# One output tile's wo product, taken in two banks at different times, and x's tiles loaded last

## The chip, the core and the metric

The kernel runs on 1 core of a Trainium2 chip. A core has TensorE (PE, matmuls; PEld are its weight loads), VectorE (DVE), ScalarE (ACT), GpSimd (POOL) and SyncE (SP), which here only issues DMAs. Matmul results go to PSUM, which has eight banks of 512 f32 columns; all else is in SBUF. The metric is the device time of one execution in microseconds (us), the median over runs; lower is better.

## The reference

A transformer block with adaptive layer norm. D = 640, 2048 rows, 32 heads of 128, a key/value cache of 2048 rows, all bf16:

```python
mod = (_silu(c) @ w_mod).reshape(c.shape[0], 6, 1, -1)      # sa, ca, ga, sb, cb, gb
h = _layernorm(x) * (1 + ca) + sa
x = x + ga * _A_ref(h, k_cache, v_cache, wq, wo)    # softmax attention, 32 heads, then @ wo
h = _layernorm(x) * (1 + cb) + sb
x = x + gb * _B_ref(h, w1, w2, w3, w4)              # x1 = x + shift4(gelu(LN(x) @ w1)) @ w2
                                                    # x1 + gelu(LN(x1) @ w3) @ w4
```

`_A_ref` projects queries with `wq`, takes softmax(q k^T / sqrt(128)) v for each head, and multiplies the 4096 concatenated values of a row by `wo` (4096 x 640). That last product, for the first rows, is what the change is about.

## The kernel before

**Planner.** Every operation is recorded by `Prog` with the tiles it reads and writes; it works out the semaphore waits. The order on each engine and on each DMA queue is the order in which the operations are recorded. A DMA that waits holds up all that stands behind it on its queue (nearly all are on SP's).

**The attention loop.** `NG` = 512 units: unit s is head s // 16, query tile s % 16 (128 rows). The loop's step s has two halves (1024 keys each). In step s, PE makes the scores of unit s (`qk`, L357 and L15: two 512-column matmuls a half, into half of `Sps`), and the product with V of unit s - 10 (`pv`, L371: eight matmuls a half). DVE copies the scores with a running minimum (L703), POOL joins the two minima (L708), ACT takes the exponential into a slot of `ring` (L711). The scores must be transposed before `pv`. Most units go three at a time (a trio) through one DMA transpose on SP (`transpose`, L286); the last trios are 491-493, 494-496, 498-500, 501-503, 504-506 and 507-509, sent at steps 493, 496, 500, 503, 506 and 510. Some units, among them 490, 497, 510 and 511, are transposed on PE instead (`t_piece`, L324: two 128x128 f32 transposes a half step, into one of the banks `JB[0]` = `Oaug` and `JB[1]` = `QPp`, or into `Sps` for 510 and 511), and ACT copies each 512-column half of the unit back to the ring (`t_evac`, L331). `PE_AT` gives the step where this starts: 501 for unit 497, and its two halves (r = 0, 1) take steps 501 and 502. The same two banks serve the query projection of the next head (`q_piece`, L301), whose last piece is in step 493.

**Values out and back.** Two units' PV results are copied by ACT (L688), normalized by POOL (L548, L555) and stored for four units at once to `o_scratch` in HBM by POOL's queue (L562). For the output product they are read back transposed: `load_ot` (L604) on SP brings a pair of query tiles, heads h0 to h1, into `OTj[pair % 2]`. Pair 0 (tiles 0 and 1) comes in four parts (`ot0(i)`, heads `OTC[i]` to `OTC[i + 1]`); parts 0, 1 and 2 are issued at the steps `OTS`, part 3 (the last head) at step 513. In step 493 and others, `ot0` of the first entry stands ahead of that step's trio on SP, the later entries behind it. `OTj[0]` lies on `hTx`, which holds the projection's input until step 493; `OTj[1]` lies on `negS`, DVE's score buffer, so pair 1 comes after the loop's last exponential.

**Output product.** Tile j's row block is `sum over heads of O_h @ wo_h`: 32 matmuls of 512 columns and 32 of 128 (`NC2`). `y0(h0, h1)` (L647) does a range of heads of tile 0 in the banks `Oaug` (512 columns) and `QPp` (128); `y1` does tile 1 in the first half of `Sps` (`a_pe`, L636). `TAIL` puts them into the loop: before, heads 0 to 15 of tile 0 go one per half step from step 504 to 511, both column parts; heads 16 to 30, and heads 0 to 30 of tile 1, follow in one block in step 513. After step 525 PE does head 31 of both tiles, then tile 2 (`a_two`, first heads 0 to 15 of pair 1, then the rest), tile 3 and so on. DVE takes each tile out of its bank (`a_s1`: L762 the product with ga, L764 the sum with x, then statistics L754, L756) and goes on with `a_s2` (L770, L773). Even tiles use the second half of `Sps`, odd ones the first.

**Loads of x.** x's 16 tiles are read again into `xt` (`load_xt`, L615): four tiles (640 KB) in step 513, between the two halves of pair 1; twelve (1920 KB) in step 522.

Of the kernel before, what the change touches and what calls it, by code (L numbers as in the profile page):

```python
# [123 lines left out]
def bass_adaLN_cond__mha_block_cached__mixer_s_mlp__prompt_kernel(  # L124
# [3 lines left out]
    _, H, SK, DH = A_k_cache.shape  # L128
# [11 lines left out]
    NG = H * NQT  # L140
# [3 lines left out]
    NC2 = [(0, 512), (512, D - 512)]  # L144

    with ExitStack() as es:
# [9 lines left out]
        if True:  # L156
            with ExitStack() as es1:
# [4 lines left out]
                PE_AT = {32 * i + t: 32 * i + a for i in range(NG // 32) for t, a in PE_T.items()}  # L162
# [97 lines left out]
                for s in range(NG):  # L260
                    end = s >= NG - 10
                    g = s - PVD
# [6 lines left out]
                    if s in first_of:  # L269
                        m = first_of[s]  # L270
                        a = take([13] if m is trios[-1] else WIN[0:3] if end else WIN)
                        for i, g in enumerate(m):
                            PSL[g] = a + i
                    if s in last_of:
                        m = last_of[s]
                        a = take([7] if m is trios[-1] else WIN[3:6] if end else WIN)
# [15 lines left out]
                def bank(key):  # L292
                    if key not in bank_of:
                        bank_of[key] = jbank[0] % 2
                        jbank[0] += 1
                    return bank_of[key]
# [14 lines left out]
                def t_bank(g, r):  # L311
                    if g >= NG - 2:
                        return Sps[:, (2 + r) * 512:(3 + r) * 512], [("S", 1), ("Sb", 2 + r)]
                    jb = bank(("t", g, r))
                    return JB[jb], [("J", jb)]

                def t_piece(g, r, q):
# [17 lines left out]
                for h in range(H):  # L335
                    pieces = {}
                    u = 2 * NQT * h
# [7 lines left out]
                    PIECES.append(pieces)  # L345

                def t_of(s):
                    return [(g, s - a) for g, a in PE_AT.items() if a <= s < a + 2]

                def qk(s, half):  # L350
                    h, j = divmod(s, NQT)
# [48 lines left out]
                for i, (n0, n1) in enumerate(MROW):  # L400
# [8 lines left out]
                     r=["id0"] + WOR, w=["ident"])  # L409
# [4 lines left out]
                     r=["c", "ident"] + WOR, w=[("J", 0)])  # L414
# [188 lines left out]
                def load_ot(pr, h0=0, h1=H, part=0):  # L603
                    G.dma("sync", lambda e: e.dma_start_transpose(  # L604
                        OTj[pr % 2][:, 2 * h0:2 * h1, :], o_scr[pr, :, h0:h1].rearrange("q h z d -> q (h z d)")),
                          ("ot", pr % 2, part), r=[("osd", pr // 2, hh) for hh in range(h0, h1)],
                          w=[("OT", pr % 2, i) for i in ([part] if pr == 0 else (part, 2)[:part + 1] if h1 - h0 < H else range(3))]
                          + ([("OTa", 0)] if pr == 2 and part == 0 else [])
                          + (HTK if pr == 0 and part == 3 else NEG if pr == 1 and part == 0 else []))

                def ot0(i):
                    load_ot(0, OTC[i], OTC[i + 1], OTP[i])

                def load_xt(c0, c1):
                    G.dma("sync", lambda e: e.dma_start(  # L615
                        xt[:, 4 * c0:4 * c1], x2d[c0 * 512:c1 * 512, :].rearrange("(t p) d -> p t d", p=128)),
                        ("xt", c0), w=[("x1", t) for t in range(4 * c0, 4 * c1)] + ringk(XT0 + 4 * c0 * D, XT0 + 4 * c1 * D))

                OTC = [0, H // 4, H // 2, H - 1, H]
                OTP = [3, 0, 1, 2]  # L620
                yn = [0]

# [17 lines left out]
                         w=[("S", b)] + ([("Sb", 2), ("Sb", 3)] if b == 1 else []))  # L640
                    return b

                def y0(h0, h1):
                    def f(t):
                        for jb, (c0, cw) in enumerate(NC2):
                            for hh in range(h0, h1):
                                ins = t.matmul(JB[jb][:, 0:cw], OTj[0][:, 2 * hh, :], wo[:, hh, c0:c0 + cw],  # L647
                                               start=(hh == 0), stop=(hh == H - 1))
                        return ins
                    G.op("tensor", f, r=[("OT", 0, OTP[i]) for i in range(4) if OTC[i] < h1 and h0 < OTC[i + 1]] + [("OTa", 0), "wo", "woz", "wo4"],  # L650
                         w=[("J", 0), ("J", 1)])

                def y1(h0, h1):
                    a_pe(1, 0, [OTP[i] for i in range(4) if OTC[i] < h1 and h0 < OTC[i + 1]], (h0, h1))
# [4 lines left out]

                YB = [Sps[:, 0:1024], Sps[:, 1024:2048]]  # L660
                LAG = 4
                Y0S = NG - 8
                OTS = [NG - 16, NG - 16, NG - 8]
                TAIL = {(s, z): [(y0, 2 * (s - Y0S) + z, 2 * (s - Y0S) + z + 1)] for s in range(Y0S, NG) for z in range(2)}
                TAIL[(NG + 1, 1)] = [(y0, OTC[2], OTC[3]), (y1, 0, OTC[3])]
                for s in range(NG + PVD + LAG):
                    h, j = divmod(s, NQT)
                    g_ = s - PVD
# [17 lines left out]
                    if 0 <= g_ < NG and g_ % 2 == 1:  # L686
# [3 lines left out]
                            r=[("O", p % 2)], w=[("Of", p % 4)])  # L690
# [4 lines left out]
                    for half in range(2):  # L695
                        if s < NG:
# [3 lines left out]
                            if is_pe(s):  # L700
# [5 lines left out]
                                r=[("S", half)], w=[("negS", s % 3), ("nmh", half, r8)])  # L706
                    if s < NG:
                        G.op("gpsimd", lambda g, r8=r8: g.tensor_scalar(  # L708
                            out=nm[:, r8:r8 + 1], in0=nm0[:, r8:r8 + 1], scalar1=nm1[:, r8:r8 + 1], scalar2=None, op0=ALU.min),
                            r=[("nmh", 0, r8), ("nmh", 1, r8)], w=[("nm", r8)])  # L710
                        G.op("scalar", lambda a, s=s, r8=r8: a.activation(  # L711
                            ring[:, PSL[s], :], negS[:, s % 3, :], ACT.Exp, bias=nm[:, r8:r8 + 1], scale=-1.0),
                            r=[("negS", s % 3), ("nm", r8)], w=slot(PSL[s]))
# [16 lines left out]
                    if 0 <= s - PVD - LAG:  # L730
                        gr, z = divmod(s - PVD - LAG, 4)
# [3 lines left out]
                    if s == NG + PVD - 9:  # L735
                        G.op("gpsimd", lambda g: g.memset(mhalf, -0.5), w=["mhalf"] + NEG)
                        ot0(3)
                        load_ot(1, 0, H // 2, 0)
                        load_xt(0, 1)
                        load_ot(1, H // 2, H, 1)  # L740
                    if s == NG + PVD:
                        load_xt(1, NQC)
                GELU = ACT.Gelu_apprx_tanh
# [273 lines left out]
```

## Time and profile before

| | us |
|---|---|
| median of 3 runs (1527.22 to 1528.97) | 1527.29 |
| the profiled execution | 1526.63 |
| its span on the core | 1524.8 |
| PE busy | 1489.2 (98%) |
| DVE busy | 1370.3 (90%) |
| ACT busy | 1256.8 (82%) |
| POOL busy | 625.9 (41%) |
| stretch 1190 to 1208: PE, DVE busy | 18.00, 18.00 |
| stretch 1208 to 1238: PE, DVE busy | 29.38, 6.40 |
| stretch 1238 to 1340: PE, DVE busy | 101.67, 69.99 |

Times within the execution count from the span's start. The granted TensorE clock was 1.00 throughout. In the timeline a row is start, length, engine, line, operation, what it writes and reads, and how many; a wait stands at its end in brackets. Lengths of PE rows overlap, since matmuls are pipelined: the price of one is the distance from start to start. Rows of SPq are the issuing of a DMA; when its data has landed is told apart (us from the issue). The chain of waits gives start, length, and what the time went to.

Step 504 begins on PE at 1189.92, step 501 at 1183.06. The last exponential begins at 1209.80, the block of heads 16 to 30 at 1211.00.

### The profile page before, as it was taken

Reading aid. Unit: us, or ns where it says so; the run is one execution under the profiler, and the core shown is the slowest. Engines: PE = TensorE matmul, PEld = TensorE weight load, DVE = VectorE, ACT = ScalarE, POOL = GpSimd, SP = SyncE. Lnnn points to the kernel's source line nnn. Section 1 sums busy time; section 2 is a strip of 40 time slices with the busy share of each in tenths; the row PEclk is TensorE's granted clock in tenths of the full one; section 3 lists DMA queues with packets and bytes.
Section 4 is the critical chain, followed back from the end, with each engine's and each line's share of the span. In section 5 each row is a group of like instructions: output and inputs, shape, how many; then the busy total and the mean of one; then the engine's idle time right before and its main releaser. Section 6 shows DMA issues by size and latency. Waiting matters only on the chain.

```text
span 1524.8 us, 32718 instructions
## 1 busy us (share of the span) xinstructions
PE 1489.2 (98%) x13702; PEld 917.9 (60%) x12678; DVE 1370.3 (90%) x2426; ACT 1256.8 (82%) x1182; POOL 625.9 (41%) x1402
## 2 busy tenths in 40 slices
PE   6899999999999999999999999999999999999999
PEld 3466666666666666666666666666666665554545
DVE  8999999999999999999999999999999756767425
ACT  6999999999999999999999999999999700034230
POOL 1244444444444444444444444444444433333000
PEclk9999999999999999999999999999999999999999
DMA  9999999999999999999999999999999998524101
GB/s 328 251 236 236 244 249 238 241 243 238 242 249 232 240 242 242 231 249 238 241 250 229 239 238 254 233 247 230 254 238 237 252 253 185 130 86 105 35 22 35
DMA packets 1155264, 330.29 MB, mean 217 GB/s; under 512 B 1133290, under 2 KB 1149738, under 8 KB 1155114
## 3 DMA queue, kind: packets, MB, share of 16 engines
q1 hardware_dynamic: 1146624, 307.09, 100.3%
q0 software_dynamic: 6144, 16.79, 3.4%
q10 hardware_dynamic: 2346, 4.34, 0.8%
q8 instruction: 103, 1.69, 0.5%
q14 instruction: 47, 0.39, 0.1%
HBM read 43.48 MB, written 19.40 MB: 41 GB/s over the span
## 4 chain that ended last, share of the span: by engine, by line
ACT 73%; PE 17%; DVE 5%; DMA 2%; issue 1%; SPq 1%; POOL 0%; DVEq 0%
ACT ring L711 60%; PE Sps L636 8%; ACT ring L331 5%; ACT Of L688 4%; ACT kv L308 4%; PE Sps L954 3%; DVE negS L703 3%; PE Oaug L905 2%; PE QPp L905 2%; PE Sps L890 1%; DMA negS<-o_scratch 1%; SPq L286 1%; DMA kv<-Of 1%; SPq L604 0%; ACT hTx L473 0%
## 5 line engine op out<-in xcount | busy, mean ns | idle before, releaser
L703 DVE TENSOR_SCALAR_CACHE_REDUCE negS<-Sps 128x1024 f32<-128x1024 f32 x1024 | 1173.9, 1223 | 8.2 <-PE Sps L15 7.3
L711 ACT ACTIVATE ring<-negS,small 128x2048 bf16<-128x2048 f32 x512 | 1116.7, 2372 | 2.1 <-POOL small L708 1.9
L371 PEld LDWEIGHTS PTp<-kv,ring 128*128 128x128 bf16 x8192 | 558.1, 98 | 295.0 <-issue 76.1
L371 PE MATMUL PTp<-kv,ring 128*128 128x129 bf16 x8192 | 645.0, 220 | 5.7 <-DMA ring<-ring 5.7
L357 PE MATMUL Sps<-kv 128*128 128x512 bf16 x1024 | 395.6, 386 | 9.0 <-DVE negS L703 4.6
L708 POOL TENSOR_SCALAR small<-small 128x1 f32<-128x1 f32 x512 | 146.1, 285 | 595.7 <-DVE negS L703 595.6
L15 PE MATMUL Sps<-kv 128*128 128x512 bf16 x1024 | 388.7, 380 | 0.0
L555 POOL TENSOR_SCALAR On<-Of,small 128x128 bf16<-128x128 f32 x512 | 190.1, 372 | 13.0
L688 ACT COPY Of<-PTp 128x259 f32<-128x259 f32 x256 | 186.3, 728 | 3.9 <-PE PTp L371 3.9
L357 PEld LDWEIGHTS Sps<-kv 128*128 128x128 bf16 x1024 | 98.3, 96 | 134.5 <-DVE negS L703 92.4
L548 POOL TENSOR_TENSOR small<-Of,small 128x4 f32<-128x4 f32 x128 | 133.1, 1040 | 13.7 <-ACT Of L688 13.5
L301 PE MATMUL Oaug<-hTx,kv 128*128 128x512 bf16 x315 | 119.0, 380 | 4.4 <-DMA kv<-in_A_wq_dram 2.6
L301 PE MATMUL QPp<-hTx,kv 128*128 128x512 bf16 x325 | 121.8, 381 | 0.9 <-ACT ring L331 0.8
L562 POOL DMA_DIRECT2D o_scratch<-On x128 | 103.8, 811 | 40.8 <-POOL On L555 37.2
L703 DVE DVE_READ_ACCUMULATOR negS<-Sps 128x1 f32 x1024 | 88.6, 87 | 0.0
L835 ACT ACT_TABLE_LOAD x1 | 1.3, 1283 | 105.9 <-POOL hTx L853 105.9
L331 ACT COPY ring<-QPp 128x512 f32<-128x512 f32 x78 | 74.9, 960 | 0.0
L331 ACT COPY ring<-Oaug 128x512 f32<-128x512 f32 x78 | 74.4, 954 | 0.0
L747 POOL TENSOR_SCALAR negS<-negS 128x1 f32<-128x1 f32 x48 | 24.3, 506 | 117.8 <-DVE negS L756 117.7
L636 PE MATMUL Sps<-wo,negS 128*128 128x128 bf16 (+1 forms) x512 | 71.5, 299 | 1.0 <-DMA negS<-o_scratch 1.0
L958 DVE TENSOR_TENSOR ring<-Sps,ring 128x640 f32<-128x640 f32 x15 | 12.4, 824 | 59.5 <-PE Sps L954 59.5
L308 ACT CAST kv<-QPp 128x512 bf16<-128x512 f32 x65 | 61.0, 938 | 1.4 <-PE QPp L301 1.4
(108 smaller groups left out, 1073.3 us busy)
## 6 DMA issues: line engine op xcount, KB each, us to landing
kv<-in_A_v_cache_dram SPq DMA_DIRECT2D x32, 512.0 KB, 5.2
o_scratch<-On POOLq DMA_DIRECT2D x128, 128.0 KB, 5.4
kv<-in_A_wq_dram SPq DMA_DIRECT2D x32, 160.0 KB, 3.5
wo<-in_A_wo_dram SPq DMA_DIRECT2D x1, 5120.0 KB, 21.5
ring<-in_A_x_dram SPq DMA_DIRECT2D x5, 640.0 KB, 5.1
ring<-in_w_mod_dram SPq DMA_DIRECT2D x5, 640.0 KB, 8.5
out_dram<-wo SPq DMA_DIRECT2D x15, 160.0 KB, 1.8
ring<-ring SPq DMA_TRANSPOSE x144, 9.6
```

The costliest lines, as they stand in the source:

```text
L15: return t.add_instruction(mybir.InstMatmult(name=t.bass.get_next_instruction_name(), ins=[t.lower_ap(rhs), t.lower_ap(lhsT)], outs=[t.low ...
L301: G.op("tensor", lambda t: t.matmul(JB[jb], wq[:, hb, q, :], hT[:, q, cc * 512:(cc + 1) * 512], start=(q == 0), stop=(q == KT - 1)), r=[(" ...
L331: G.op("scalar", lambda a: a.copy(dst, src), r=keys[-1:], w=[("PT", TSL[g], r)])
L357: ins = (t.matmul if c2 == 0 else partial(same_weights, t))(Sps[:, col:col + 512], QT[:, hb, j * 128:(j + 1) * 128], KTs[:, hb, col:col + ...
L371: ins = t.matmul(ob[:, 0:129], pt, Vaug[:, hb, kt, 0:129], start=(kt == 0), stop=(kt == NKT - 1))
L548: G.op("gpsimd", lambda g: g.tensor_tensor(out=rl[:, 4 * b:4 * b + 4], in0=Of[:].rearrange("p a z d -> p (a z) d")[:, 4 * b:4 * b + 4, 128 ...
L555: G.op("gpsimd", lambda g: g.tensor_scalar(out=On[:, b, z, :], in0=Of[:, 2 * b + z // 2, z % 2, 0:128], scalar1=rl[:, 4 * b + z:4 * b + z ...
L636: ins = t.matmul(YB[b][:, c0:c0 + cw], OTj[pr % 2][:, 2 * hh + z, :], wo[:, hh, c0:c0 + cw], start=(hh == 0), stop=(hh == H - 1))
L688: G.op("scalar", lambda a, p=p: a.copy(Of[:, p % 4].rearrange("p z d -> p (z d)")[:, 0:259], PO[:, (p % 2) * 512:(p % 2) * 512 + 259]), r= ...
L703: G.op("vector", lambda v, half=half, dst=dst, src=src, r8=r8: v.tensor_scalar(out=dst, in0=src, scalar1=-SCALE, scalar2=None, op0=ALU.mul ...
L708: G.op("gpsimd", lambda g, r8=r8: g.tensor_scalar(out=nm[:, r8:r8 + 1], in0=nm0[:, r8:r8 + 1], scalar1=nm1[:, r8:r8 + 1], scalar2=None, op ...
L711: G.op("scalar", lambda a, s=s, r8=r8: a.activation(ring[:, PSL[s], :], negS[:, s % 3, :], ACT.Exp, bias=nm[:, r8:r8 + 1], scale=-1.0), r= ...
```

## The change

- Tile 0's sums run at different times in the two banks. The 512-column part takes heads 0 to 23, one per half step, in steps 499 to 510; the 128-column part takes heads 0 to 13, one per half step, in steps 505 to 511. The block in step 513 then does heads 14 to 23 of the 128-column part, heads 24 to 30 of both, and heads 0 to 30 of tile 1.
- `OTC` cuts pair 0 into 16, 8, 7 and 1 heads (before: 8, 8, 15 and 1). Part 0 is issued at step 493 (before 496), part 1 at 496, part 2 at 504 as before.
- Since `Oaug` is taken from step 499 on, unit 497 uses `QPp` alone: its first half is transposed in step 501, the second in step 503 (before: 501 and 502, in two banks).
- On SP, pair 1's second half is issued before x's first four tiles.

```diff
                 def t_bank(g, r):
                     if g >= NG - 2:
                         return Sps[:, (2 + r) * 512:(3 + r) * 512], [("S", 1), ("Sb", 2 + r)]
-                    jb = bank(("t", g, r))
+                    jb = 1 if g == NG - 15 else bank(("t", g, r))
                     return JB[jb], [("J", jb)]
...
                 def t_of(s):
-                    return [(g, s - a) for g, a in PE_AT.items() if a <= s < a + 2]
+                    return [(g, (s - a) // (1 + (g == NG - 15))) for g, a in PE_AT.items()
+                            if s in ((a, a + 2) if g == NG - 15 else (a, a + 1))]
...
-                OTC = [0, H // 4, H // 2, H - 1, H]
+                OTC = [0, H // 2, 3 * H // 4, H - 1, H]
...
-                def y0(h0, h1):
+                def y0(h0, h1, jbs=(0, 1)):
                     def f(t):
-                        for jb, (c0, cw) in enumerate(NC2):
+                        for jb in jbs:
+                            c0, cw = NC2[jb]
                             for hh in range(h0, h1):
...
-                         w=[("J", 0), ("J", 1)])
+                         w=[("J", jb) for jb in jbs])
...
-                Y0S = NG - 8
-                OTS = [NG - 16, NG - 16, NG - 8]
-                TAIL = {(s, z): [(y0, 2 * (s - Y0S) + z, 2 * (s - Y0S) + z + 1)] for s in range(Y0S, NG) for z in range(2)}
-                TAIL[(NG + 1, 1)] = [(y0, OTC[2], OTC[3]), (y1, 0, OTC[3])]
+                OTS = [NG - 19, NG - 16, NG - 8]
+                YU = (2 * NG - 26, 2 * NG - 14)
+                TAIL = {divmod(u, 2): [(y0, u - YU[i], u - YU[i] + 1, (i,)) for i in range(2) if 0 <= u - YU[i] < OTC[2]]
+                        for u in range(YU[0], 2 * NG)}
+                TAIL[(NG + 1, 1)] = [(y0, 2 * NG - YU[1], OTC[2], (1,)), (y0, OTC[2], OTC[3]), (y1, 0, OTC[3])]
...
                         load_ot(1, 0, H // 2, 0)
+                        load_ot(1, H // 2, H, 1)
                         load_xt(0, 1)
-                        load_ot(1, H // 2, H, 1)
```

## The prediction

> **What bounds the kernel now.** The page first: ACT falls to 7 tenths in slice 32 of 40 and to 0 in 33 to 35, while PE stays at 9, so the attention loop ends near 1210 us and a PE-bound part follows. The edit lies around that seam, so I read the chain of waits there.
>
> ```profile
> 1203.51 2.32 DVE negS L703 x4
> ...
> 1213.95 6.50 SPq L286
> 1220.51 1.25 SPq L604
> 1221.81 5.70 SPq L604
> 1228.18 10.11 DMA negS<-o_scratch
> 1238.33 102.32 PE Sps L636 x752
> ```
>
> To be seen: DVE (the score copies) sets the loop's pace to its end; then SP's queue of DMA transposes carries the chain up to pair 1's second half, and at 1238.33 it hands over to PE, whose 752 matmuls follow without a hole. So time is won only if PE gets to that point sooner, which needs both PE and the transposes. Next the timeline of PE.
>
> ```profile
> 1183.97 0.39 PE L324 MATMUL Oaug<-identf,ring 128*128 128x128 f32 x2
> ...
> 1190.83 0.38 PE L647 MATMUL Oaug<-wo,hTx 128*128 128x512 bf16 x1
> 1191.05 0.22 PE L647 MATMUL QPp<-wo,hTx 128*128 128x128 bf16 x1
> ...
> 1211.00 3.40 PE L647 MATMUL Oaug<-wo,hTx 128*128 128x512 bf16 x15
> 1214.23 1.00 PE L647 MATMUL QPp<-wo,hTx 128*128 128x128 bf16 x15
> ...
> 1232.87 4.51 PE L636 MATMUL Sps<-wo,negS 128*128 128x512 bf16 x32
> 1238.33 7.97 PE L636 MATMUL Sps<-wo,negS 128*128 128x512 bf16 x48 [0.95 <-DMA negS<-o_scratch]
> ```
>
> To be seen: durations overlap, so prices are start-to-start. 15 matmuls of 512 columns take 3.23 us (1211.00 to 1214.23), 0.215 each; of 128 columns 0.84, 0.056 each. From 1189.92 to 1237.38 PE has no hole; then it waits 0.95 for pair 1. Last, SP's queue and two lines of DVE.
>
> ```profile
> 1168.45 0.58 SPq L231 DMA_DIRECT2D kv<-in_A_v_cache_dram  x1
> 1171.58 6.33 SPq L286 DMA_TRANSPOSE ring<-ring  x1
> 1177.95 2.59 SPq L604 DMA_TRANSPOSE hTx<-o_scratch  x1
> 1180.64 6.24 SPq L286 DMA_TRANSPOSE ring<-ring  x1
> 1186.92 2.47 SPq L604 DMA_TRANSPOSE hTx<-o_scratch  x1
> ...
> 1202.46 4.34 SPq L604 DMA_TRANSPOSE hTx<-o_scratch  x1
> ...
> 1227.55 0.58 SPq L615 DMA_DIRECT2D ring<-in_A_x_dram  x1
> 1228.18 6.07 SPq L604 DMA_TRANSPOSE negS<-o_scratch  x1
> ```
>
> ```profile
> 1233.72 0.83 DVE L764 TENSOR_TENSOR ring<-ring 128x640 bf16<-128x640 f32 x1
> 1243.48 0.89 DVE L773 SCALAR_TENSOR_TENSOR ring<-ring,negS,mod_bc 128x640 f32<-128x640 f32 x1 [4.31 <-DMA ring<-in_A_x_dram]
> ```
>
> To be seen: SP is free from 1169.03 to 1171.58 (it waits for step 493's exponential) and then issues back to back up to 1234.9. x's first transfer (L615) stands ahead of pair 1's second half.
>
> **Part 1, the sums in the loop.** A half step on PE is two score matmuls 0.44, eight PV 0.465, together 0.905. Two transposes of a PE tile add 0.23 (1183.97 to 1184.20), a 512-column sum 0.215, a 128-column one 0.05. DVE takes 1.145 for a half (2.29 a step). Before, steps 501 and 502 have transposes (1.135, under DVE), 503 nothing, 504 to 511 both sums (1.17: PE bound, 0.025 late each half; after 14 halves PE has used up its lead of 0.36 and DVE first starts 0.02 late, at 1206.97).
> After: 499 and 500 hold one 512 sum, 1.12 a half, still under 1.145, so DVE hides these four (0.86 us of PE work that leaves the full stretch). Steps 501 and 503 hold transposes and a sum, 1.35: 0.41 late each; 502 and 504 give back 0.05 each; 505 to 510 lose 0.025 twelve times. Sum 0.41-0.05+0.41-0.05+0.30 = 1.02, less the lead of 0.36: DVE ends the loop about 0.65 later. PE itself, which is then never idle from step 501 on, is the count that matters: from 1183.06 (score of 501) to 1237.38 it had 0.51 us of holes (6.86 us for steps 501 to 503, against 6.35 of work). These go, and the 0.86 goes: PE reaches pair 1's second half 1.37 sooner, at 1236.0. The bulk at 1211 loses eight 512 matmuls (1.72) and gains two of 128 (0.11).
>
> The 0.215 is this trace's row. The Trainium skill, TensorE: Matmul & The Clock Gate, section Back-to-back issue gap, gives about 131 ns for a matmul of 512 columns in a stream with weight loads; by it the four that leave would be worth 0.52, and the time 0.34 us more. Its isolated gap of 216 ns is the one that this trace shows.
>
> **Part 2, tile 497 in one bank.** Its second half is transposed at step 503 in place of 502, in the bank that its first half used. PE then waits for ACT's copy: that of the first half begins at 1186.72 and takes 0.6, PE comes at 1188.9: 1.6 of room. The second copy stands ahead of the exponential of 503 (1191.7), the first 128-column sum comes at 1193.9. ACT has these copies two steps apart, with work of 2.0 and 0.6 against two steps of 2.29. Tile 497 is read at step 507. ACT's slack hides it, cost 0; without that cover PE, which paces here, would pay each us in full.
>
> **Part 3, SP's queue.** Same number of transfers; 16, 8, 7 heads for 8, 8, 15. The first is issued at 493, ahead of the trio 491 to 493, as soon as PE's last projection (1166.80) is done: at 1169.1. No row has 16 heads there: 5.0 us by twice 2.5, 6.07 by the row of pair 1. I take 5.0, the same source and tile. The trio then starts at 1174.1, 2.5 late. That trio landed 7.9 us after its issue, others in this stretch 8.7 to 9.7; its transfer runs behind another, so I take 9.4: 1183.5. Tile 491's PV want it at 1183.50. Between the ends (1182.0, and 1184.9 with 6.07 and 9.7) the stall is 0 to 1.4, at the taken value 0. It would be paid in full, as PE is behind from there on. The next trio starts at 1180.5 as before (1180.64). From step 500 on SP is 0.3 early, after the 7 heads (2.1 for 4.34) 2.5 early. Nothing else gates it: exponential 509 ends at 1207.8 with the 0.65, SP comes at 1211.4. POOL's store of head 31 (issued 1211.10, landed 1216.16) moves with DVE to 1216.8, SP wants it at 1218.1.
> The sums' inputs: 16 heads land by 1169.1+5.0+2.8 = 1176.9 (8 heads landed 2.7 to 3.4 after the issue's end), the first sum is at 1179.4; the 8 by 1192.7 for 1198; the 7 by 1207 for 1211.7.
>
> **Part 4, x last.** Pair 1's second half goes 0.63 ahead of x: with the 2.5, issued at 1225.1 and landed 7.6 (first half) to 10.1 us (its own row) later: 1232.7 to 1235.2. Both are under PE's 1236.0, so the 0.95 wait goes too. x is issued at 1231.2 and lands 4.4 us later at the least (1235.6), at most 9.0 (the large x transfer): 1240.2. DVE's first add (L764, 1233.72 before) waits; behind it in DVE's order are tile 0's statistics and the product that frees tile 1's bank, 2.7 us in all (1233.72 to 1236.40), and PE's tile 3 waits for that bank, at 1238.33+4.4-2.3 = 1240.4. So x may land up to 1237.7 for nothing. Nearest row: x landed 2.5 after the transposes ahead of it (1231.96 after 1229.45), here 1235.2 to 1237.7. Cost 0; ends 0 and 2.5. The large x transfer follows at 1231.8, 2.5 sooner than 1234.35, so the 4.31 wait on DVE does not grow.
>
> **Sum.** PE passes 1238.33 at 1236.0: -2.3 us (1.37 + 0.95). Then the loop over tiles is PE's (DVE waits 32.2 us for PE in it), so it reaches the end. Profiled execution 1526.63 (span 1524.8) to 1524.3; the median shown, 1527.29, lies 0.66 above, so 1525.0.
>
> **Rivals.**
> - Trio late: the stall of part 3, up to 1.4. For it, no margin at the taken values; against, the one trio issued after a pause landed in 7.9. Time 1525.7 (1525.2 to 1526.4). Chance 0.14.
> - Transposes set the end: SP's gain is eaten by the transfers themselves (from 1174 to 1178 packets move at 290 GB/s without a gap, so the queue may be held by the engines), and pair 1 comes only 0.63 sooner. 1526.7. Chance 0.10.
> - The other side, x too late: mechanism of part 4. At 1240.0 all is given back, from 1243.1 it is slower by 0.2%. For it, 1920 KB follow 0.6 us behind on the same queue; against, the 4.4 row. At 9.0: 1527.5; if the two x transfers share the engines to the end (2560 KB in 13.4 us by 4.4 and 9.0), x lands at 1244.6 and the time is 1531.9. The Trainium skill, DMA: Bandwidth & Descriptors, section Queues, rings and completion order, says each DMA engine takes descriptors in ring order; by that rule x waits for pair 1 but not for the large transfer, and the landings 1229.45, 1231.96, 1238.29, 1243.36 in the order of issue agree. Chance 0.12, of which 0.07 beyond 0.2%.
> - More gain: PE's later holes (0.5 on a transposed tile and 0.2 on ACT, in the mixer) close as well: 1524.3 or less. For it, both hang on DVE's pace in the tiles; against, they lie 140 us on, behind work that PE paces. Chance 0.12.
> - The forecast, 1525.0 (1524.4 to 1525.7): 0.52.
>
> **Numbers.** 0.2% is 3.05 us, about what a measurement here can tell from none; so the forecast itself is "same". Faster needs 1524.24: 0.08 of the 0.12 for more gain, and 0.11 of the forecast by the spread of runs (1527.22 to 1528.97): 0.19. Slower: 0.07 from x, and 0.06 from the first two rivals should they meet and a run lie high: 0.13. Same 0.68. The range 1524.0 to 1527.6 leaves out about 0.06 below and 0.12 above.
>
> **What would show it.** Sums into Oaug from step 499 (about 1179), steps 501 and 503 longer by 0.4 on PE, DVE's last score copy near 1208.8; 16 heads in one L604 of about 5 us before the trio of 493; the bulk sums at 1211 with 7 and 17 matmuls; no wait on pair 1; L764 waiting for x instead of L773. Wrong, if PE shows a hole at tile 491 or 494, or before tile 3, or if the time after tile 2 changes.

## The result and the profile after

| | before | after |
|---|---|---|
| median of 20 runs each, on one chip (us) | 1527.73 | 1530.64 |
| ratio, 95% interval | | 1.0015 [1.0008, 1.0022] |
| the profiled execution, its span (us) | 1526.63, 1524.8 | 1531.31, 1529.5 |

Slower by 0.15%: inside the 0.2% that the prediction calls "same", but on the other side of zero from the forecast of -2.3 us, and above its range (1524.0 to 1527.6).

The profiled execution after is already 2.3 us later than the one before at step 490, ahead of anything that the change touches: its granted clock had been 0.50 for 6.8 us at 16.7 and for 3.4 us at 1078.2. The first is no difference: the record of the clock before begins at 22.5 only, and scores took 0.63 there too up to 22.2 (0.38 from then on), so the 1.00 told above holds from 22.5. The second stands behind a 2.0 us wait for a trio, which is 1.1 in the kernel before and has no half clock behind it. So both are compared from the start of DVE's first copy of step 490 (1158.88 before, 1161.20 after); "t" below is the time since then, worked out so for every kernel.

| t of | before | after | difference |
|---|---|---|---|
| DVE's copy of step 501 | 25.18 | 25.18 | 0 |
| DVE's last score copy | 49.26 | 52.12 | +2.86 |
| PE begins tile 1's block | 56.20 | 57.03 | +0.83 |
| PE begins tile 4 | 92.50 | 93.50 | +1.00 |
| PE begins tile 6 | 109.89 | 112.93 | +3.04 |
| PE begins tile 14 | 179.44 | 182.70 | +3.26 |
| end of the span | 365.95 | 368.30 | +2.35 |

The chain of waits, after (start, us, what):

```profile
1176.89 1.04 ACT ring L714
1177.93 10.10 DMA ring<-ring
1188.08 0.64 PE PTp L372 x8
...
1235.91 5.41 PE Sps L637 x38
1241.32 13.33 DMA hTx<-o_scratch
...
1254.70 4.52 PE Sps L637 x32
...
1262.48 11.60 DMA negS<-o_scratch
...
1274.13 4.06 PE Sps L637 x18
```

Before, the chain had one handover from a transfer to PE, at 1238.33. Now there are three: the trio 491-493, pair 2 (`hTx`) and pair 3 (`negS`). PE's timeline, after:

```profile
1188.08 0.64 PE L372 MATMUL PTp<-kv,ring 128*128 128x129 bf16 x8 [2.08 <-DMA ring<-ring]
...
1216.54 1.46 PE L649 MATMUL Oaug<-wo,hTx 128*128 128x512 bf16 x6
1217.83 0.55 PE L649 MATMUL QPp<-wo,hTx 128*128 128x128 bf16 x7
...
1254.70 17.56 PE L637 MATMUL Sps<-wo,hTx 128*128 128x512 bf16 x126 [1.14 <-DMA hTx<-o_scratch]
1274.13 2.12 PE L637 MATMUL Sps<-wo,negS 128*128 128x512 bf16 x9 [1.87 <-DMA negS<-o_scratch]
```

Pair 1's wait of 0.95 is gone. In its place stand 2.08 at tile 491, 1.14 at tile 4 and 1.87 at tile 6. The block's 512-column matmuls cost 0.215 each as before (1216.54 to 1217.83 for six). SP's queue, after:

```profile
1170.54 0.58 SPq L231 DMA_DIRECT2D kv<-in_A_v_cache_dram  x1
1171.16 6.67 SPq L605 DMA_TRANSPOSE hTx<-o_scratch  x1
1177.93 13.13 SPq L286 DMA_TRANSPOSE ring<-ring  x2
...
1235.74 5.53 SPq L616 DMA_DIRECT2D ring<-in_A_x_dram  x2
1241.32 14.67 SPq L605 DMA_TRANSPOSE hTx<-o_scratch  x2
1256.04 0.58 SPq L860 DMA_DIRECT2D kv<-in_B_w_dram  x1
1256.66 0.52 SPq L861 DMA_DIRECT2D negS<-in_B_w_dram  x1
1261.24 1.20 SPq L793 DMA_TRANSPOSE kv<-Of  x1
1262.48 8.04 SPq L605 DMA_TRANSPOSE negS<-o_scratch  x1
```

Two rows matter. The 16 heads (L605 at 1171.16) hold SP for 6.67 us, and the trio goes out behind them (L286 at 1177.93, two trios in one row). And the two x transfers (L616) take 5.53 us of SP where issuing them takes about 1: SP stands until the first has landed (1240.89). SP's own waits from 1230 to 1265 say so:

```profile
SPq L616 <- DMA ring<-in_A_x_dram: 4.5, 1, 4.5
SPq L109 <- DMA kv<-in_B_w_dram: 4.0, 1, 4.0
```

The reason is in the planner's keys, not in the data. x's tiles 0 to 3 end, and tile 4 begins, inside the same ring slot, and a slot is one key: the second x transfer is a write after a write on the first. With x between pair 1's halves, 6.1 us of issuing lay between the two, and the first had landed when SP came to the second. Side by side, the wait is laid open, and pair 2 stands behind it. The second line is the same kind: the transposition of tile 0's next input (L793) waits for w1's landing, since they share a key, and pair 3 stands behind that. The kernel before stands there as well (4.2 us); there it cost PE nothing.

### The profile page after: what moved, and what is told of

Its sections match the earlier page's. It is cut to its first block, busy times and chain, and to the rows that moved or that the text cites. A ratio compares the mean times of both kernels' runs of the same rounds, so it can differ in the third digit from the quotient of the medians.

```text
span 1529.5 us, 32477 instructions
## 1 busy us (share of the span) xinstructions
PE 1470.9 (96%) x13463; PEld 918.1 (60%) x12678; DVE 1371.3 (90%) x2426; ACT 1258.3 (82%) x1182; POOL 628.4 (41%) x1402
## 3 DMA queue, kind: packets, MB, share of 16 engines
q10 hardware_dynamic: 2346, 4.34, 0.8%
## 4 chain that ended last, share of the span: by engine, by line
ACT 68%; PE 21%; DVE 5%; DMA 4%; issue 2%; POOL 0%; ACTq 0%; SPq 0%; POOLq 0%
ACT ring L714 55%; PE Sps L637 7%; ACT ring L331 4%; ACT Of L691 4%; DVE negS L706 4%; ACT kv L308 4%; PE Sps L957 3%; DMA ring<-ring 2%; PE QPp L908 2%; PE Oaug L908 2%; PE PTp L372 2%; PE Sps L893 1%; DMA hTx<-o_scratch 1%; DMA negS<-o_scratch 1%; PE Oaug L830 1%
## 5 line engine op out<-in xcount | busy, mean ns | idle before, releaser
L706 DVE TENSOR_SCALAR_CACHE_REDUCE negS<-Sps 128x1024 f32<-128x1024 f32 x1024 | 1174.8, 1224 | 12.7 <-PE Sps L15 10.7
L15 PE MATMUL Sps<-kv 128*128 128x512 bf16 x1006 | 381.9, 380 | 9.2 <-DVE negS L706 5.9
L358 PE MATMUL Sps<-kv 128*128 128x512 bf16 x961 | 371.4, 387 | 13.9 <-DVE negS L706 1.9
L691 ACT COPY Of<-PTp 128x259 f32<-128x259 f32 x256 | 209.0, 816 | 5.7 <-PE PTp L372 5.7
L549 POOL TENSOR_TENSOR small<-Of,small 128x4 f32<-128x4 f32 x128 | 133.3, 1041 | 10.9 <-ACT Of L691 10.6
L301 PE MATMUL Oaug<-hTx,kv 128*128 128x512 bf16 x254 | 96.4, 381 | 5.6 <-DMA kv<-in_A_wq_dram 3.9
L301 PE MATMUL QPp<-hTx,kv 128*128 128x512 bf16 x263 | 97.6, 378 | 1.1 <-ACT ring L331 0.8
L331 ACT COPY ring<-QPp 128x512 f32<-128x512 f32 x79 | 81.6, 1032 | 0.3 <-PE QPp L324 0.3
L331 ACT COPY ring<-Oaug 128x512 f32<-128x512 f32 x77 | 80.7, 1048 | 0.0
L308 ACT CAST kv<-QPp 128x512 bf16<-128x512 f32 x65 | 66.6, 1025 | 0.6 <-PE QPp L301 0.6
```

The source lines that it names most:

```text
L15: return t.add_instruction(mybir.InstMatmult(name=t.bass.get_next_instruction_name(), ins=[t.lower_ap(rhs), t.lower_ap(lhsT)], outs=[t.low ...
L301: G.op("tensor", lambda t: t.matmul(JB[jb], wq[:, hb, q, :], hT[:, q, cc * 512:(cc + 1) * 512], start=(q == 0), stop=(q == KT - 1)), r=[(" ...
L331: G.op("scalar", lambda a: a.copy(dst, src), r=keys[-1:], w=[("PT", TSL[g], r)])
L358: ins = (t.matmul if c2 == 0 else partial(same_weights, t))(Sps[:, col:col + 512], QT[:, hb, j * 128:(j + 1) * 128], KTs[:, hb, col:col + ...
L549: G.op("gpsimd", lambda g: g.tensor_tensor(out=rl[:, 4 * b:4 * b + 4], in0=Of[:].rearrange("p a z d -> p (a z) d")[:, 4 * b:4 * b + 4, 128 ...
L691: G.op("scalar", lambda a, p=p: a.copy(Of[:, p % 4].rearrange("p z d -> p (z d)")[:, 0:259], PO[:, (p % 2) * 512:(p % 2) * 512 + 259]), r= ...
```

## The experiments

Two questions: what the trio's wait comes from, and what the waits of pairs 2 and 3 come from. A result is the median, then the ratio to the kernel before on the same chip with its 95% interval.

### x back between pair 1's halves

**x_first**, the changed kernel with only this part undone:

```diff
                         load_ot(1, 0, H // 2, 0)
-                        load_ot(1, H // 2, H, 1)
                         load_xt(0, 1)
+                        load_ot(1, H // 2, H, 1)
```

> The changed kernel with x's first four tiles back between the halves of pair 1; the rest of the change stays. Theory A (two faults, both on SP: 16 heads ahead of the trio 491 to 493, and x's second transfer, which waits on SP for the first one to land because tile 4 begins in the ring slot where tile 3 ends): the first fault stays (PE waits about 2 us at tile 491), the second goes, since the first x transfer lands before SP reaches the second; PE no longer waits for pairs 2 and 3 (1.1 and 1.9 us), and waits 0 to 1 us for pair 1. Time about 2.5 us under the changed kernel, 1528.1. Theory B (the sums in the loop are too dense, and the tail only shows that): nothing comes back, 1530.6 or a little more. Theory C (x late on DVE costs, by tile 3's bank): the time falls by what PE waits before tile 3 alone, near 0.

1530.13 us, 1.0004 [0.9996, 1.0013]. No wait at pairs 1, 2 or 3: the waits at tiles 4 and 6 are x's. (Pair 1 is no gain of this order: its second half landed at t = 80.3, and PE came at 81.2, 2.0 later than in the changed kernel.) The trio's wait stays, 2.86, and shows a second cost. Busy time by stretch (the number behind POOL is the granted clock):

```profile
1180.00:1190.00 10.00, 7.29 (x66) 4.15 (x59) 9.06 (x16) 9.98 (x8) 4.38 (x10) 0.98 1.28 236
1190.00:1192.00 2.00, 1.71 (x12) 1.36 (x12) 0.00 (x0) 0.33 (x1) 0.00 (x0) 0.50 1.28 290
1192.00:1194.00 2.00, 2.00 (x15) 0.98 (x12) 0.92 (x1) 0.45 (x2) 0.00 (x0) 0.77 1.28 290
```

PE's wait ends at 1190.29; from 1189.5 the clock is 0.50 for 3.4 us.

### x last, alone

**x_last_only**, the kernel before with only x moved:

```diff
                         load_ot(1, 0, H // 2, 0)
-                        load_xt(0, 1)
                         load_ot(1, H // 2, H, 1)
+                        load_xt(0, 1)
```

> The kernel before with the order on SP's queue alone changed: pair 1's second half, then x. Theory A: pair 1 comes some 2 us sooner (the 0.95 us wait goes), but SP then stands about 4.5 us before x's second transfer, pairs 2 and 3 land about 4 us later, and PE waits 1 to 3 us in all at tiles 4 and 6: 1528 to 1530 against 1527.7 before. Theory B: pair 1's wait goes and nothing else, 1526.8. Theory C: PE waits at tile 3 and not at 4 or 6.

1531.89 us, 1.0015 [1.0006, 1.0023]: this one moved line costs as much as the whole change. Its waits of PE (us in total, times, longest) and its SP queue:

```profile
PE Sps L636 <- DMA negS<-o_scratch: 2.2, 1, 2.2
PE Sps L636 <- DMA hTx<-o_scratch: 1.7, 1, 1.7
```

```profile
1234.43 5.52 SPq L615 DMA_DIRECT2D ring<-in_A_x_dram  x2
1239.99 15.21 SPq L604 DMA_TRANSPOSE hTx<-o_scratch  x2
```

Pair 1's 0.95 is won, and 3.9 lost at pairs 2 and 3. The profiled execution ends 5.1 later than the kernel before; 1.7 of that is a clock of 0.50 for 3.4 us from 1274.4, behind the wait at tile 6 (tile 7 begins 10.4 after tile 6, before 8.7).

### The second x transfer freed

**x_unlock**, the changed kernel with other keys for it (the first x transfer's slot is no longer named):

```diff
-  ... + ringk(XT0 + 4 * c0 * D, XT0 + 4 * c1 * D))
+  ... + ringk(3 * SK if c0 else XT0, XT0 + 4 * c1 * D))
```

> The changed kernel, but x's second transfer no longer claims the ring slot that it shares with the first (its earlier users are done when the first is issued, on the same queue). Theory A: SP does not stand there; the second x transfer is issued at once behind the first, pairs 2 and 3 land about 4.3 us sooner, PE waits for neither: 3.0 us under the changed kernel, 1527.6; the wait of 2 us at tile 491 stays. Theory B: no more than 0.5 us. Theory C: two x transfers side by side make the first land later, PE waits longer before tile 3, no gain.

1530.61 us, 1.0003 [0.9993, 1.0014]. By its ratio that is 1.8 us under the changed kernel, not the 3.0 expected. The second x transfer goes out 0.6 us behind the first, pair 2 lands at t = 92.1 (93.5 in the changed kernel, where PE wanted it at 92.4), and tile 4 no longer waits. But pair 3 lands at 113.0, no sooner than in the changed kernel (112.9): SP still stands 4.4 us for w1 at L793 ahead of it. Tile 6 waits 0.77 only, since PE comes later. The trio's wait is 2.62, with half clock behind it.

### x last with all three orders taken away

**x_last_free**, `x_last_only` with that and two more: the product of tile 0 names only the slot that it writes, and L793 no longer claims the space that w1 is loaded to.

```diff
-  ... + ringk(XT0 + 4 * c0 * D, XT0 + 4 * c1 * D))
+  ... + ringk(3 * SK if c0 else XT0, XT0 + 4 * c1 * D))
...
-                TMPK = ringk(0, 4 * D)
+                TMPK = ringk(0, SK)
...
-                    n_t(j, l == 1 and j == 0)
+                    n_t(j, False)
```

> The kernel before with x's first four tiles behind pair 1's second half, as in the change, and with three orders taken out by other places and keys: x's second transfer names no ring slot that the first writes, the product of tile 0 names its own slot alone, and the first transposition of nT does not wait for w1's landing. Pair 0's parts and the sums are as before. Theory (the move of x itself is good, and only the shared slot made it bad): no wait at pair 1, none over 0.5 us at tiles 4 and 6, span 0.6 to 1.2 us below before's, ratio 0.9990 to 0.9998 against 1.0015 for the move alone. Rival (the transfers behind pair 1 are late because the queues and the memory are full, whatever x's order): waits of 1 to 2 us at tiles 4 or 6 again, ratio 1.0005 to 1.0020.

1527.12 us, 0.9992 [0.9982, 1.0002], against 1.0015 for the move alone. Its SP queue:

```profile
1233.67 1.13 SPq L615 DMA_DIRECT2D ring<-in_A_x_dram  x2
1234.85 15.50 SPq L604 DMA_TRANSPOSE hTx<-o_scratch  x2
```

The x transfers take 1.13 of SP, not 5.52, and PE waits for none of pairs 1 to 3. The end is at t = 365.00, 0.95 before the kernel before: as much as the wait that the prediction wanted to win. So moving x did harm only through the recorded orders. This run takes all three away together. With the slot alone freed, x_unlock still waits at pair 3, so what each order is worth by itself stays open.

### The parts of pair 0 alone

**before_parts**, the kernel before with the new parts and steps, sums and x where they were:

```diff
-                OTC = [0, H // 4, H // 2, H - 1, H]
+                OTC = [0, H // 2, 3 * H // 4, H - 1, H]
...
-                OTS = [NG - 16, NG - 16, NG - 8]
+                OTS = [NG - 19, NG - 16, NG - 8]
...
-                TAIL[(NG + 1, 1)] = [(y0, OTC[2], OTC[3]), (y1, 0, OTC[3])]
+                TAIL[(NG + 1, 1)] = [(y0, OTC[1], OTC[3]), (y1, 0, OTC[3])]
```

> The kernel before with the change's division of pair 0's transfer alone: 16 heads behind step 493, 8 behind step 496, 7 behind step 504. The sums stay in the order of before (both column blocks of heads 0 to 15 from step 504, heads 16 to 30 behind the loop), and x stays between pair 1's halves. Theory (the eight more heads ahead of trio 491-493 are what delays it): TensorE stands 1.5 to 3.0 us at tile 491 with a DMA of the ring as releaser, although no sum has moved; pair 1's wait of about 0.95 us stays; ratio 1.0007 to 1.0020. Rival (the sums moved into steps 499 to 511 delay the trio, by the work that they add on TensorE or ScalarE): no wait over 0.5 us at tile 491; ratio 0.9995 to 1.0005.

1528.90 us, 1.0008 [1.0000, 1.0017]. SP's queue and PE's wait:

```profile
1168.86 0.58 SPq L231 DMA_DIRECT2D kv<-in_A_v_cache_dram  x1
1169.49 6.73 SPq L604 DMA_TRANSPOSE hTx<-o_scratch  x1
1176.31 12.47 SPq L286 DMA_TRANSPOSE ring<-ring  x2
```

```profile
PE PTp L371 <- DMA ring<-ring: 1.0, 3, 0.6
```

The trio is late without any moved sum, but by less than expected: 0.59 at tile 491 and 0.22 at two later ones. The trio landed 8.6 us after its issue, not 10.1. Pair 1's wait, which was expected to stay, is gone: its second half landed at t = 77.2 (79.4 before), and PE came at 79.6.

### V elsewhere

The load of head 31's V stands just ahead of the 16 heads. **v_early** is the changed kernel with it one trio sooner (step 489), **before_v_early** the kernel before with the same edit:

```diff
+                        if s == NG - 23:
+                            load_v(H - 1)
...
-                        if j == PVD + 1 and h + 1 < H:
+                        if j == PVD + 1 and h + 2 < H:
```

> The changed kernel, with the load of head 31's V one transposed trio sooner on SP (ahead of the trio 487 to 489, which has several us of room, instead of behind it), so that V's 512 KB do not run beside the 16 heads. x as in the changed kernel. Theory A1 (the 16 engines of the DMA are the limit in steps 489 to 506; V's transfer only has to find idle time, and there is some before the 16 heads): the 16 heads take about 5 us, the trio 491 to 493 lands before step 501, PE's 2 to 3 us at tile 491 go. The time gains less than that, since x's lock still holds pairs 2 and 3: their waits grow from 3.0 to some 4. About 0.1% under the changed kernel. Theory A2 (the eight heads pulled forward are what the DMA has no room for, wherever V stands): PE still waits 1 us or more at tile 491, 494 or 498.

> Control: the kernel before with V's load moved in the same way. All theories: no difference from before (V has 15 steps of room in both places), so that what the last runs gain is not V's own.

v_early: 1530.25 us, 1.0016 [1.0003, 1.0028], the trio's wait is 2.13, as in the changed kernel, and tile 6 waits 2.62, with 3.4 us at a clock of 0.50 behind it (from 1270.5). before_v_early: 1528.38 us, 1.0005 [0.9994, 1.0016], traces as before (0.99 at pair 1). V went sooner, but the trio 487-489 behind it then took 7.4 us of SP instead of 5.9, and the 16 heads went out at t = 11.6, after 10.0 in the changed kernel. V's 512 KB are in the way of the trio from either place.

**v_early_x_unlock** is v_early with x_unlock's keys, **best** is that with the other two lines of x_last_free:

> The same, and x's second transfer without the shared ring slot. Theory A1: no wait in the loop, none at tile 4, under 1 us at tile 6; the loop's end as predicted, 1.3 us before that of the kernel before on PE: 0.1% faster than before. Theory A2: as the run with V behind the trio (1.1 us at a trio), no difference from before.

> The same, and two more claims taken off that hold a queue up though the bytes are apart: DVE's product of tile 0 no longer claims the ring slot where x's tile 0 begins (it waited for x), and the first transposed tile of the second layer norm no longer waits on SP for w1 to land, with pair 3 behind it. Theory A1: PE waits nowhere between step 499 and tile 14; 2.3 us under the kernel before (0.15%), what was predicted for the change. Theory A2: the trio's wait remains, about 1.5 us under before.

1528.42 us, 0.9996 [0.9983, 1.0008], and 1528.12 us, 0.9995 [0.9987, 1.0004]. Freeing x takes v_early from 1.0016 to 0.9996, with no wait left at pairs 1 to 3. The trio's wait stays (2.16 and 2.97).

**x_unlock_v_later** is x_unlock with V behind the trio 491-493:

```diff
-                        if j == PVD + 1 and h + 1 < H:
+                        if j == PVD + 1 + 2 * (h == H - 2) and h + 1 < H:
```

> As the last, and the load of head 31's V goes behind the trio 491 to 493 on SP (it stood ahead of the 16 heads; tile 496 needs it at step 506). Theory A, with the cause that the 16 heads took 6.67 us on SP because V's 512 KB ran beside them: they take about 5.0, the trio is issued 2.3 us sooner and lands before tile 491 is wanted, PE's wait of 2 us goes, and the time is 1525.5, what was predicted for the change. If the 16 heads take 6.6 us by themselves: the trio is issued 0.6 us sooner, the wait falls to 1.4 us, 1527.0.

1528.74 us, 0.9996 [0.9987, 1.0006]. Its SP queue, and its PE where it waits:

```profile
1169.08 4.89 SPq L605 DMA_TRANSPOSE hTx<-o_scratch  x1
1174.07 6.33 SPq L286 DMA_TRANSPOSE ring<-ring  x1
1180.45 0.58 SPq L231 DMA_DIRECT2D kv<-in_A_v_cache_dram  x1
1181.13 8.82 SPq L286 DMA_TRANSPOSE ring<-ring  x1
```

```profile
1193.25 0.64 PE L372 MATMUL PTp<-kv,ring 128*128 128x129 bf16 x8 [1.10 <-DMA ring<-ring]
```

Without V ahead, the 16 heads hold SP for 4.89 (the prediction took 5.0), and the trio is there in time, at t = 22.9. But now the next trio stands behind V, takes 8.82 instead of about 6.3, and tile 494 waits 1.10. The wait only moved on. PE waits 0.19 at pair 1, 0.55 at tile 3 and 0.83 at tile 6 besides.

The trio 491-493 in the kernel before and in those with 16 heads ahead of it (t, from each trace's SP rows and landings; tile 491 wants it at t = 24.6 to 25.1, in pad_64 at 25.8):

| kernel | V issued | 16 heads on SP (us) | trio issued | trio landed | PE's wait |
|---|---|---|---|---|---|
| before | 9.6 | (none there) | 12.7 | 20.6 | 0 |
| after | 9.3 | 6.7 | 16.7 | 26.8 | 2.08 |
| x_first | 10.2 | 6.8 | 17.7 | 27.6 | 2.86 |
| x_unlock | 10.1 | 6.7 | 17.5 | 27.3 | 2.62 |
| v_early | 3.4 | 5.2 | 16.8 | 26.9 | 2.13 |
| v_early_x_unlock | 3.2 | 5.4 | 16.9 | 26.9 | 2.16 |
| best | 3.8 | 5.6 | 17.6 | 27.7 | 2.97 |
| x_unlock_v_later | 20.7 | 4.9 | 14.3 | 22.9 | 0 (1.10 at tile 494) |
| before_parts | 9.3 | 6.7 | 16.8 | 25.4 | 0.59 (1.0 in three) |
| pad_64 | 10.6 | 6.7 | 18.0 | 27.5 | 1.76 |
| pad_96 | 9.7 | 7.0 | 17.5 | 27.4 | 2.35 |

### The instruction transfers

Why did the trio need 10.1 us with the early sums and 8.6 without? In the changed kernel one queue more is at work while it is under way. The DMA view of 1184.5 to 1187.5, after (packets, MB, share of 16 engines):

```profile
q8 instruction: 1, 0.02, 2.2%
```

That 16 KB transfer begins at t = 24.6, and the transposes' packets fall from about 1130 a us to 88 in the us from 1186.2. In before_parts it begins at t = 30.2, behind the trio, and in x_unlock_v_later, which has the early sums and whose trio also took 8.6, at 26.0, behind it too. **pad_64** and **pad_96** move it: the changed kernel with 64 or 96 small products, unused, at the very start, where PE stands 6.7 us for weights.

```diff
+                def pad(t):
+                    for _ in range(64):
+                        ins = t.matmul(JB[1][:, 0:KT], c_row, ident[0:KT, 0:KT], start=True, stop=True)
+                    return ins
+                G.op("tensor", pad, r=["c", "ident"] + WOR, w=[("J", 1)])
```

> The changed kernel with 64 small TensorE products (5 by 5, result unused) at the very start, where TensorE stands 6.7 us for the first weights. They add 128 instructions and nothing else, so every later 16 KB instruction transfer should come about 128 of TensorE's instructions sooner: in the changed kernel one began 24.6 us behind the vector engine's first copy of step 490, in the middle of trio 491-493; here it should begin near 17 to 18 us. Theory (that transfer stops the trio's stream and makes about 1.5 us of the 2.1 us wait): trio 491-493 lands 8 to 9.3 us after its issue (10.1 in the changed kernel), TensorE's wait at tile 491 falls to 0.3 to 1.4 us. Rival (the wait comes from the eight more heads and V alone, and the instruction transfer only happens to be there): landing after 9.8 to 10.2 us, wait 1.8 to 3.0 us. The waits of x's order at tiles 4 and 6 stay in both; ratio 1.0000 to 1.0012 by the theory, 1.0008 to 1.0022 by the rival.

> As pad_64 with 96 small products: 192 instructions, so the transfers near 24.6 us should fall near 14 us and near 29 to 31 us, behind the trio's landing. Theory: the trio lands 8 to 9.3 us after its issue, wait at tile 491 of 0.3 to 1.4 us; the next trio, 494-496, is met by the later transfer and may give a wait of up to 1 us at tile 494. Rival: landing after 9.8 to 10.2 us and a wait of 1.8 to 3.0 us at tile 491, whatever the instruction transfers do.

1529.82 us, 1.0012 [1.0002, 1.0022], and 1527.70 us, 0.9998 [0.9988, 1.0007]. The transfers moved, to t = 19.2 and 17.2, but the trio still landed 9.5 and 10.0 us after its issue, with waits of 1.76 and 2.35 at tile 491. By the expectation the theory that this transfer makes most of the wait falls: pad_96 is as its rival said, and pad_64 lies between the two. The traces show why a shift of that size could not settle it: the hole in the stream now lies in the 16 heads, which land at t = 21.5 and 20.9 (18.8 in the changed kernel) and let the first sum wait for them, 0.92 and 0.25. The transposes from V to the trio are one stream without slack, and that a hole anywhere in it delays its end is only argued. Why before_parts lands its trio 1.5 us sooner than the changed kernel, from the same issue, stays open.

The pads show one thing more. SP still stands for x in both (3.6 and 3.9 us), yet pair 2 lands at t = 92.2 and 91.1, and tile 4, which PE begins at 92.9 and 92.8, does not wait (tile 6 does in pad_64, 0.73, and does not in pad_96). In the changed kernel it landed at 93.5. The lock's price hangs on 1 to 2 us of slack.

### A later third part

**late_part** keeps the change's aim and lets the trio 491-493 go: pair 0 in five parts, the first two as before, heads 16 to 23 behind the trio 498-500; the 512-column sums start at step 501 with 22 heads in the loop; x freed as in x_last_free.

```diff
-                OTC = [0, H // 2, 3 * H // 4, H - 1, H]
-                OTP = [3, 0, 1, 2]
+                OTC = [0, H // 4, H // 2, 3 * H // 4, H - 1, H]
+                OTP = [3, 0, 1, 4, 2]
...
-                OTS = [NG - 19, NG - 16, NG - 8]
-                YU = (2 * NG - 26, 2 * NG - 14)
+                OTS = [NG - 16, NG - 16, NG - 12, NG - 8]
+                YU = (2 * NG - 22, 2 * NG - 14)
...
```

> The changed kernel with pair 0 in five parts: heads 0 to 7 and 8 to 15 where the kernel before has them (step 496), heads 16 to 23 behind trio 498-500 (step 500), heads 24 to 30 behind step 504, head 31 last. The 512-column sums begin at step 501 (22 heads in the loop), the 128-column sums at step 505 (14 heads). x's transfers are freed as in x_last_free. Theory (both late transfers of the change have one cause each, and without them its gain on TensorE shows): no wait at tile 491, none at pairs 1 to 3, at most 0.6 us at tile 501, whose trio goes 2.2 us later; span 1.2 to 2.3 us below before's, ratio 0.9985 to 0.9993. Rival (eight heads ahead of any trio cost a wait, since every trio from 491 on lands just in time): 1.5 to 2.5 us at tile 501, with half clock behind it perhaps; ratio 0.9995 to 1.0010.

1526.43 us, 0.9990 [0.9981, 0.9998]: a little faster than the kernel before, and faster than the changed one; from x_last_free (0.9992) it can't be told apart. SP's queue and all waits of PE from 1150 to 1300:

```profile
1173.05 6.26 SPq L286 DMA_TRANSPOSE ring<-ring  x1
1179.35 2.37 SPq L605 DMA_TRANSPOSE hTx<-o_scratch  x1
...
1191.34 6.40 SPq L286 DMA_TRANSPOSE ring<-ring  x1
1197.78 3.15 SPq L605 DMA_TRANSPOSE hTx<-o_scratch  x1
1200.98 6.38 SPq L286 DMA_TRANSPOSE ring<-ring  x1
```

```profile
PE Sps L15 <- DVE negS L706: 0.6, 2, 0.3
PE Sps L637 <- DMA negS<-o_scratch: 0.4, 1, 0.4
```

The trio 491-493 goes out at t = 12.7 and lands at 20.5, as before. The one that is now pushed (501-503, issued at 1200.98) comes in time. The end is at t = 364.30, 1.65 before the kernel before and 0.7 before x_last_free.

That 0.7 is not shown to be the sums'. They bring PE to tile 1's block 0.44 sooner (t = 55.76 for 56.20), but pair 1's second half lands at 78.5, and PE waits 0.43 for it. At tile 14 late_part is 0.73 ahead of the kernel before, x_last_free 0.90. The 0.7 comes after that, in the mixer, where x_last_free stands 0.69 at t = 220.1 for a transposed tile and late_part does not: the same transposition landed 7.8 us after its issue there, 6.2 here. Why is open. All five kernels with the sums as before have this wait (0.37 to 0.83), and of the ten with early sums pad_64 alone (0.68).

## Why the prediction was wrong, by its steps

**Part 1, the sums: right.** DVE's last copy was to come 0.65 later. It came 2.86 later, of which the trio's wait is 2.08: 0.78. In late_part, which has no such wait and 22 heads in the loop, it is 0.75. PE was to gain 1.37: tile 1's block begins 0.83 later with a wait of 2.08 ahead of it, so 1.25 was gained. The price of a 512-column matmul, 0.215, held; 131 ns, the figure of the Trainium skill (TensorE: Matmul & The Clock Gate, Back-to-back issue gap), is not what this trace shows.

**Part 2, tile 497 in one bank at 0: right.** No wait of PE for ACT's copies shows.

**Part 3, SP's queue: wrong, in two terms of one sum.** "I take 5.0" for the 16 heads measured 6.67, above the upper end of 6.07. The working took twice the row of 8 heads, but that row has no V load ahead of it; with V behind, 4.89 was measured. "so I take 9.4" for the landing measured 10.1, again above its end. Together the trio came 2.2 later than taken, and the stall of 0 (0 to 1.4) was 2.08. The same step's "after the 7 heads (2.1 for 4.34) 2.5 early" failed too: pair 1's first half went out at t = 64.1, after 62.9 before. The 7 heads did take less (2.52 for 4.34), but the two trios behind them took as much of SP as ever, 6.62 and 7.30, after 6.95 and 6.50. By these rows SP's times are not a price list of independent parts: with more ahead of it in the stream, a transpose holds the queue longer. That was the ground of the rival "Transposes set the end", given 0.10.

**Part 4, x last: wrong, and where it came true partly by luck.** Pair 1's second half was to land at 1232.7 to 1235.2 (t = 73.8 to 76.3), under PE's 1236.0 (77.1). It landed at t = 78.1, after 79.4 before, and its 0.95 wait went only because the trio's wait had made PE late (79.2). Without that wait PE would have come at 77.1 and stood about 1.0 here, an estimate from these rows; in late_part, with no trio's wait, it did stand 0.43. So by these rows about -1.4 was to be had at this point (78.1 for 79.5), not -2.3. The step that made the change slower is one sentence, "The large x transfer follows at 1231.8, 2.5 sooner than 1234.35". The first x transfer now stands right ahead of it, the two share a slot, and SP stood 4.5 us for the first to land. Pair 2, behind it on SP, went out at t = 80.1, after 76.0; pair 3 stood behind L793 in turn. Waits of 1.14 and 1.87 where the working had none. The working asked who waits for x's data, on DVE, and not who waits for x on SP. DVE did wait long for x (26.4 us), not at the sum with x as the working had it but at L765, the product of tile 0, whose recorded slots include one of x's. In x_unlock_v_later it cost 0.55 at tile 3; in the changed kernel it cost nothing:

```profile
1240.99 0.69 DVE L765 TENSOR_TENSOR ring<-Oaug,mod_bc 128x512 f32<-128x512 f32 x1 [26.44 <-DMA ring<-in_A_x_dram]
```

**The sum.** -1.25 (sums) - 0.95 (pair 1) + 2.08 (trio) + 1.14 + 1.87 (pairs 2 and 3) make +2.9; tile 14 measured +3.26, the rest in gaps under 0.25. Of this 0.9 comes back in the later part, 0.55 of it by a wait at 1379.9 that the kernel before has and the changed one has not; the end is +2.35, and the ratio of 1.0015 is +2.3.

**The rivals.** "Trio late" named the first loss and its place, with up to 1.4 for it. "The other side" had x as its cause, but by x's landing at tile 3, not by the queue behind it. Each was priced alone, and both losses happened. "Transposes set the end" is what late_part shows at pair 1, once the others are away. "More gain" came half true: the hole of 0.5 in the mixer closed, that of 0.2 stayed.

## What to carry to other kernels

When a DMA is moved on a queue, read its recorded keys against its new neighbour: a buffer slot that two transfers share at an edge is a wait that lies hidden as long as other issues stand between them, and all that is behind on the queue pays. A trio that lands 4 us ahead of its use has 4 us of slack for all that is put ahead of it, and the price is taken from a row with the same transfers in front, not from the same transfer elsewhere. Where an early load is needed, put it behind a transfer that still has slack, as late_part does, and check that PE does not lose the time won at the next transfer, as it did there at pair 1.

## What was not expected of the hardware

- **Half clock behind a short wait.** In x_first, x_unlock, v_early_x_unlock and best, PE's wait of 2.2 to 3.0 us at the trio was followed by 3.4 us at a granted clock of 0.50, and in x_last_only and v_early that of 2.2 and 2.6 at tile 6; scores took 0.63 instead of 0.38 (x_first). With waits at the trio alike (2.13 and 2.16), v_early without it there begins tile 1 at t = 57.05, v_early_x_unlock with it at 58.73: 1.7 us more. The changed kernel's own 2.08 was not followed by it, nor pad_96's 2.35. The length of the wait does not decide alone. In every trace the changes of the granted clock lie whole multiples of 3.413 us apart. In the stretch between two such marks just before a half clock PE was busy 22 to 43% (x_first 39%, from 1186.1), counting from 35 us on in all 15 traces, and no stretch with 46% or more was followed by one (v_early's trio 46%, pad_96's 50%, the changed kernel's 57%). So in these traces a wait of 2 us or more has this price or not by how it falls between the marks, and these lie elsewhere in each execution. In the first 35 us the two groups overlap.
- **Instruction transfers in the transposes' way.** A 16 KB transfer on q8 comes every 9 to 20 us in this stretch, and the transposes' stream, 1130 packets of 256 bytes a us, breaks for 1 to 2 us around it in these traces (88 packets in the us from 1186.2). Where it falls moves with the count of PE's instructions ahead, as the pads show.
